# Layer scale on one core: all loads on one DMA ring, all stores on the other, and a first load cut in two

## The chip, the core and the metric

The kernel runs on one core of a Trainium2 chip. Times are device microseconds (us) of one execution. The kernel before takes 121.36 us, the median of 10 runs between 121.07 and 121.44.

## The reference

```python
B, S, D = 1024, 16, 512          # x, y: [B, S, D] bf16; gamma: [D] bf16

def reference(x, y, gamma):
    return x + gamma * y
```

Both inputs and the output are 16,384 rows of 512 bf16 numbers, 16.8 MB each. So 33.6 MB are read from HBM and 16.8 MB written to it, with one multiplication and one addition per element.

## The kernel before

Partition p of 128 holds the rows 128p to 128p + 127 (the rearranged views `xv`, `yv`, `ov`, L38 to L40). The 128 rows of a partition are cut into four pieces of 32 (`PIECE`, L5). One piece is a transfer of 128 partitions with 32 x 512 x 2 bytes = 32 KB each, in all 4 MB. `y_sb` (L45) holds all four pieces of y and later the results, in place; x has two buffers of one piece, `xs` (L46), used in turn.

No scheduler or pool is at work: each engine's order is the order in which the code issues to it, and every wait is written by hand with semaphores. `_take` (L9) waits until a semaphore has reached n and takes n off again.

- **gamma.** ACT loads the row (L65). TensorE multiplies it with a column of ones, so that it stands in all 128 partitions of PSUM (L69), and VectorE (DVE in the profile) copies it into `gamma_sb` (L71).
- **SP's DMA ring** (L75 to L83): x0, x1; then, each after a wait on `s_sp`, x2 and x3 into the buffers that the adds of pieces 0 and 1 have freed; the store of piece 0; after a further wait the store of piece 2.
- **ACT's DMA ring** (L86 to L93): gamma, y0, y1, y2, y3, and, each after a wait on `s_act`, the stores of pieces 1 and 3.
- **VectorE** (L95 to L113), for each piece: wait for y, multiply it by `gamma_sb` in place (L98), wait for x and for the multiplication, add x (L104). The end of the add is told to SP or ACT.
- At the end SP waits for both rings' stores (L115, L116).

The gamma load and the loads x0, x1, y0 and y1 are in the list `first`. L118 to L124 move these instructions to the head of the program, ahead of the barrier with which all engines start.

Of the kernel before, what the change touches and what calls it, by code (L numbers as in the profile page):

```python
# [3 lines left out]

PIECE = 32  # L5
MULT, ADD = mybir.AluOpType.mult, mybir.AluOpType.add


def _take(sem, n, eng):  # L9


    return eng.wait_ge(sem, n).then_inc(sem, -n)  # L12


def kernel(
    tc: tile.TileContext,
    x: bass.AP,
    y: bass.AP,
    gamma: bass.AP,
    out: bass.AP,  # L20
):

    nc = tc.nc
    P = nc.NUM_PARTITIONS
    tc.close()
    tc.compile()  # L29

    xf = x.flatten_outer_dims()
    yf = y.flatten_outer_dims()
    of = out.flatten_outer_dims()
    N, D = xf.shape
    rows = N // P
    n = rows // PIECE
    dt = xf.dtype
    xv = xf.rearrange("(p n) d -> p n d", p=P)  # L38
    yv = yf.rearrange("(p n) d -> p n d", p=P)
    ov = of.rearrange("(p n) d -> p n d", p=P)  # L40

    gamma_row = nc.alloc_sbuf_tensor("gamma_row", [1, D], dt).ap()
    ones_row = nc.alloc_sbuf_tensor("ones_row", [1, P], dt).ap()
    gamma_sb = nc.alloc_sbuf_tensor("gamma_sb", [P, D], dt).ap()
    y_sb = nc.alloc_sbuf_tensor("y_sb", [P, rows, D], dt).ap()  # L45
    xs = [nc.alloc_sbuf_tensor(f"x{i}", [P, PIECE, D], dt).ap() for i in range(2)]  # L46
    gamma_ps = nc.alloc_psum_tensor("gamma_ps", [P, D], mybir.dt.float32).ap()

    sem = nc.alloc_semaphore
    s_gamma, s_ones, s_ps, s_dve = sem("s_gamma"), sem("s_ones"), sem("s_ps"), sem("s_dve")  # L50
    s_x = [sem(f"s_x{c}") for c in range(n)]
    s_y = [sem(f"s_y{c}") for c in range(n)]
    s_sp, s_act = sem("s_sp"), sem("s_act")
    s_out_sp, s_out_act = sem("s_out_sp"), sem("s_out_act")

    def piece(c):
        return slice(c * PIECE, (c + 1) * PIECE)

    first = []

    def load(eng, dst, src, s):
        return eng.dma_start(out=dst, in_=src).then_inc(s, 16)


    first.append(load(nc.scalar, gamma_row, gamma.unsqueeze(0), s_gamma))  # L65
    nc.vector.memset(ones_row, 1.0).then_inc(s_ones, 1)  # L66
    _take(s_ones, 1, nc.tensor)
    _take(s_gamma, 16, nc.tensor)
    nc.tensor.matmul(gamma_ps, ones_row, gamma_row, start=True, stop=True).then_inc(s_ps, 1)  # L69
    _take(s_ps, 1, nc.vector)  # L70
    nc.vector.tensor_copy(out=gamma_sb, in_=gamma_ps).then_inc(s_dve, 1)  # L71
    _take(s_dve, 1, nc.vector)


    first.append(load(nc.sync, xs[0], xv[:, piece(0), :], s_x[0]))  # L75
    first.append(load(nc.sync, xs[1], xv[:, piece(1), :], s_x[1]))
    _take(s_sp, 1, nc.sync)
    load(nc.sync, xs[0], xv[:, piece(2), :], s_x[2])
    _take(s_sp, 1, nc.sync)
    load(nc.sync, xs[1], xv[:, piece(3), :], s_x[3])  # L80
    nc.sync.dma_start(out=ov[:, piece(0), :], in_=y_sb[:, piece(0), :]).then_inc(s_out_sp, 16)
    _take(s_sp, 1, nc.sync)
    nc.sync.dma_start(out=ov[:, piece(2), :], in_=y_sb[:, piece(2), :]).then_inc(s_out_sp, 16)  # L83


    for c in range(n):  # L86
        i = load(nc.scalar, y_sb[:, piece(c), :], yv[:, piece(c), :], s_y[c])
        if c < 2:
            first.append(i)
    _take(s_act, 1, nc.scalar)  # L90
    nc.scalar.dma_start(out=ov[:, piece(1), :], in_=y_sb[:, piece(1), :]).then_inc(s_out_act, 16)
    _take(s_act, 1, nc.scalar)
    nc.scalar.dma_start(out=ov[:, piece(3), :], in_=y_sb[:, piece(3), :]).then_inc(s_out_act, 16)  # L93

    for c in range(n):  # L95
        yt = y_sb[:, piece(c), :]
        _take(s_y[c], 16, nc.vector)
        nc.vector.tensor_tensor(  # L98
            out=yt, in0=yt, in1=gamma_sb[:, None, :].to_broadcast([P, PIECE, D]), op=MULT
        ).then_inc(s_dve, 1)  # L100
        _take(s_x[c], 16, nc.vector)
        _take(s_dve, 1, nc.vector)

        i = nc.vector.tensor_tensor(out=yt, in0=xs[c % 2], in1=yt, op=ADD)  # L104
        if c == 0:
            i.then_inc(s_sp, 1)
        elif c == 1:
            i.then_inc(s_dve, 1)
            _take(s_dve, 1, nc.vector)
            nc.vector.sem_inc(s_sp, 1)  # L110
            nc.vector.sem_inc(s_act, 1)
        else:
            i.then_inc(s_sp if c == 2 else s_act, 1)  # L113

    _take(s_out_sp, 32, nc.sync)  # L115
    _take(s_out_act, 32, nc.sync)  # L116

    main = nc.main_func.blocks[0].instructions  # L118
    names = {i.ins.name for i in first}
    for b in nc.main_func.blocks[1:]:  # L120
        for i in [i for i in b.instructions if i.name in names]:
            b.instructions.remove(i)
    for k, i in enumerate(first):
        main.insert(1 + k, i.ins)  # L124


# [1 line left out]
_INS = ['x', 'y', 'gamma']  # L128
_OUTS = [((1024, 16, 512), 'bfloat16')]


# [23 lines left out]
```

## Time and profile before

| What | Value |
|---|---|
| median of 10 runs | 121.36 us |
| the profiled execution's own time | 121.14 us |
| its span, first to last instruction | 119.8 us |
| VectorE busy | 70.3 us (59%) |
| four multiplications (L98), each | 8.691 us |
| four additions (L104), each | 8.692 us |
| VectorE idle ahead of its first multiplication | 18.0 us |
| moved by DMA | 50.33 MB, 420 GB/s over the span |
| share of 16 DMA engines, SP's ring and ACT's ring | 50.0% and 48.7% |

In the profile the queue q1 is SP's ring and q10 is ACT's. "DMA" in the view by slices is the busy share of the core's 16 DMA engines in tenths, and the GB/s below it are credited to the slice in which a packet starts, which is why they swing from slice to slice. A view by stages gives for each stretch of time the busy time of TensorE, of its weight load, of VectorE and of GpSimd, with the number of instructions, then the granted TensorE clock, the DMA share and GB/s. In the view by time each line has its start and its length in us; a DMA line has the length of the issuing instruction, not that of the transfer.

### The profile page before, as it was taken

What the parts mean: (1) busy time and instruction counts of PE and PEld (TensorE: products, weight loads), DVE (VectorE), ACT (ScalarE), POOL (GpSimd) and SP (SyncE); (2) the same over time, 40 slices, a digit from 0 to 9 for tenths busy, and PEclk for the clock granted to TensorE, in tenths of its full rate; (3) what the DMA queues carried; (4) which work ended last, traced back from release to release, by engine and by line L of the source; (5) the groups of instructions that cost most, each with busy time, mean ns of one, the idle gap of its engine ahead of it and who ended that gap; (6) DMA issues with size and microseconds to landing.
All of it is one profiled execution on the core that took longest, in us unless ns stands there. A gap on an engine that the chain in (4) does not pass through costs nothing. (4 is left out here: it accounts for less than half of the span.)

```text
span 119.8 us, 90 instructions
## 1 busy us (share of the span) xinstructions
PE 0.6 (0%) x1; PEld 0.1 (0%) x1; DVE 70.3 (59%) x10; POOL 0.2 (0%) x4
## 2 busy tenths in 40 slices
PE   0100000000000000000000000000000000000000
PEld 0000000000000000000000000000000000000000
DVE  0100000099999999999899999899999700000000
POOL 0000000000000000000000000000000000000000
DMA  8989898989898989898998989899999898989895
GB/s 263 438 383 492 372 503 361 514 361 514 350 525 350 525 350 525 350 492 383 438 438 383 492 361 438 350 427 427 449 416 460 383 492 361 503 361 503 372 481 219
DMA packets 1730, 50.33 MB, mean 420 GB/s; under 512 B 193, under 2 KB 194, under 8 KB 194
## 3 DMA queue, kind: packets, MB, share of 16 engines
q1 hardware_dynamic: 864, 25.17, 50.0%
q10 hardware_dynamic: 866, 25.17, 48.7%
HBM read 33.56 MB, written 16.78 MB: 420 GB/s over the span
## 5 line engine op out<-in xcount | busy, mean ns | idle before, releaser
L98 DVE TENSOR_TENSOR y_sb<-y_sb,gamma_sb 128x16384 bf16<-128x16384 bf16 x4 | 34.8, 8691 | 18.8 <-DVEq L12 18.8
L104 DVE TENSOR_TENSOR y_sb<-x,y_sb 128x16384 bf16<-128x16384 bf16 x4 | 34.8, 8692 | 0.6
L71 DVE CAST gamma_sb<-gamma_ps 128x512 bf16<-128x512 f32 x1 | 0.7, 692 | 2.7 <-DVEq L12 2.7
L66 DVE MEMSET ones_row<- 1x128 bf16 x1 | 0.2, 165 | 2.7 <-PEq L29 2.7
L69 PE MATMUL gamma_ps<-gamma_row,ones_row 1*128 1x512 bf16 x1 | 0.6, 579 | 4.8 <-PEq L12 4.8
L69 PEld LDWEIGHTS gamma_ps<-gamma_row,ones_row 1*128 1x128 bf16 x1 | 0.1, 100 | 4.8 <-issue 4.8
L139 POOL MEMSET const-bfloat16-1.0<- 128x1 bf16 x1 | 0.1, 102 | 0.0
L139 POOL MEMSET const-uint8-127<- 128x1 uint8 x1 | 0.1, 102 | 0.0
L139 POOL MEMSET const-float32-0.0<- 128x1 f32 x1 | 0.1, 99 | 0.2 <-issue 0.2
L139 POOL MEMSET const-float32-1.0<- 128x1 f32 x1 | 0.1, 99 | 0.0
## 6 DMA issues: line engine op xcount, KB each, us to landing
x<-in_x_dram SPq DMA_DIRECT2D x4, 4096.0 KB, 24.8
y_sb<-in_y_dram ACTq DMA_DIRECT2D x4, 4096.0 KB, 47.1
out_dram<-y_sb ACTq DMA_DIRECT2D x2, 4096.0 KB, 30.3
out_dram<-y_sb SPq DMA_DIRECT2D x2, 4096.0 KB, 42.1
gamma_row<-in_gamma_dram ACTq DMA_DIRECT2D x1, 1.0 KB
```

What stands on the lines that cost most here:

```text
L66: nc.vector.memset(ones_row, 1.0).then_inc(s_ones, 1)
L69: nc.tensor.matmul(gamma_ps, ones_row, gamma_row, start=True, stop=True).then_inc(s_ps, 1)
L71: nc.vector.tensor_copy(out=gamma_sb, in_=gamma_ps).then_inc(s_dve, 1)
L98: nc.vector.tensor_tensor(out=yt, in0=yt, in1=gamma_sb[:, None, :].to_broadcast([P, PIECE, D]), op=MULT).then_inc(s_dve, 1)
L104: i = nc.vector.tensor_tensor(out=yt, in0=xs[c % 2], in1=yt, op=ADD)
L139: nc = _bacc.Bacc("TRN2", target_bir_lowering=False, num_devices=1)
```

## The change

The two rings get lists, `SP` and `ACT`, that a function `ring` works off in order. An x entry has its rows and its place in the buffer `x_sb`, which takes the place of the two x buffers and has their size.

- SP's ring carries all loads: x0, y0, x1, y1, y2, x2, y3, x3. x2 waits for the first add, x3 for the second (a count in `s_add`, one for each add).
- ACT's ring carries gamma and all four stores. The first store also names piece 2, so it waits until three adds are done; stores 1 and 2 follow without a further wait, store 3 waits for the fourth add.
- All stores count on one semaphore, `s_out`, and SP waits once for 64. The adds all count on `s_add`; ACT adds 1 to `s_end` when it has issued its last store.
- The first load of x is two transfers: the partitions 0 to 15 (`FIRST = 16`) and the partitions 16 to 127. Both count on the same semaphore, and the first add waits for 32 on it.
- Ahead of the start barrier stand both parts of x0, y0 and gamma. x1 and y1 are issued behind it.
- VectorE's computing instructions and their order are the same.

The core of the diff:

```diff
-PIECE = 32
+PIECES = [32, 32, 32, 32]
+SP = [('x', 0, 32, 0), ('y', 0, 32), ('x', 32, 64, 32), ('y', 32, 64), ('y', 64, 96), ('x', 64, 96, 0), ('y', 96, 128), ('x', 96, 128, 32)]
+ACT = [('g',), ('s', 0, 32, 2), ('s', 32, 64), ('s', 64, 96), ('s', 96, 128)]
+EARLY = (2, 1)
+FIRST = 16
...
-    xs = [nc.alloc_sbuf_tensor(f"x{i}", [P, PIECE, D], dt).ap() for i in range(2)]
+    x_sb = nc.alloc_sbuf_tensor("x_sb", [P, x_rows, D], dt).ap()
...
+    def ring(eng, what, n_early):
+        known, went = 0, False
+        for k, w in enumerate(what):
+            kind = w[0]
+            need = frees(w) if kind == "x" else pieces_of(w[1], w[2]) + list(w[3:]) if kind == "s" else []
+            need = max((order[c] + 1 for c in need), default=0)
...
+            if need > known:
+                eng.wait_ge(s_add, need)
+                known = need
...
+            elif kind == "x":
+                to = x_sb[:, w[3] : w[3] + w[2] - w[1], :]
+                r = slice(w[1], w[2])
+                if w == x_loads[0]:
+                    i = eng.dma_start(out=to[:FIRST], in_=xv[:FIRST, r, :])
+                    early.append(i.then_inc(s_load[w], 16).ins)
+                    i = eng.dma_start(out=to[FIRST:], in_=xv[FIRST:, r, :])
+                else:
+                    i = eng.dma_start(out=to, in_=xv[:, r, :])
+                i.then_inc(s_load[w], 16)
...
+            else:
+                r = slice(w[1], w[2])
+                i = eng.dma_start(out=ov[:, r, :], in_=y_sb[:, r, :]).then_inc(s_out, 16)
...
+    ring(nc.sync, SP, EARLY[0])
+    ring(nc.scalar, ACT, EARLY[1])
...
-    _take(s_out_sp, 32, nc.sync)
-    _take(s_out_act, 32, nc.sync)
+    nc.scalar.sem_inc(s_end, 1)
+    _take(s_end, 1, nc.sync)
+    _take(s_add, n, nc.sync)
+    _take(s_out, 16 * len(stores), nc.sync)
```

## The prediction

> **What bounds the kernel now.** I read the activity by slices first, then the queues, the stages, and the instructions in order of time.
>
> ```profile
> DMA  8989898989898989898998989899999898989895
> GB/s 263 438 383 492 372 503 361 514 361 514 350 525 350 525 350 525 350 492 383 438 438 383 492 361 438 350 427 427 449 416 460 383 492 361 503 361 503 372 481 219
> ...
> q1 hardware_dynamic: 864, 25.17, 50.0%
> q10 hardware_dynamic: 866, 25.17, 48.7%
> ```
>
> The DMA engines are busy in every slice from the first to the last. The shares of the two queues (SP's and ACT's) add up to 98.7% of 16 engines over 119.8 us, 118.2 us for each engine. The stages say the same; the columns that matter are the DMA share and GB/s at the end of each line.
>
> ```profile
> 0.00:3.00 3.00, 0.00 (x0) 0.00 (x0) 0.17 (x1) 0.20 (x4) 1.00 0.81 262
> 3.00:41.00 38.00, 0.58 (x1) 0.10 (x1) 17.33 (x3) 0.00 (x0) 1.00 1.01 435
> 41.00:60.00 19.00, 0.00 (x0) 0.00 (x0) 18.41 (x4) 0.00 (x0) 1.00 1.01 436
> 60.00:73.00 13.00, 0.00 (x0) 0.00 (x0) 12.85 (x2) 0.00 (x0) 1.00 0.96 413
> 73.00:77.00 4.00, 0.00 (x0) 0.00 (x0) 4.00 (x1) 0.00 (x0) 1.00 1.12 385
> 77.00:96.00 19.00, 0.00 (x0) 0.00 (x0) 17.55 (x3) 0.00 (x0) 1.00 0.99 428
> 96.00:117.00 21.00, 0.00 (x0) 0.00 (x0) 0.00 (x0) 0.00 (x0) 1.00 1.01 437
> 117.00:119.80 2.80, 0.00 (x0) 0.00 (x0) 0.00 (x0) 0.00 (x0) 1.00 0.44 187
> ```
>
> Loads alone (3 to 41 us) run at 435 GB/s, stores alone (96 to 117) at 437, the mixed middle no faster. So neither direction nor mixture matters. One packet is one partition's piece, 32x512 bf16 = 32 KB, and the trace's packet records last 1.213 us in the median, on both queues; call that P. Each of 16 engines has 96 packets (50.33 MB / 32 KB / 16): 96 x 1.213 = 116.4 us. The span is 119.8. The other 3.4 us: the first packet starts 1.0 us after the first instruction, the first round takes some 1.8 us in place of 1.2 (+0.6), packets between 72 and 76 us lose about 1.0, and about 0.8 goes to ends of transfers and the last completion. The loads and the multiply-adds pass each other here:
>
> ```profile
> 24.22 8.69 DVE L98 TENSOR_TENSOR y_sb<-y_sb,gamma_sb 128x16384 bf16<-128x16384 bf16 x1 [18.00 <-DVEq L12]
> 33.06 8.69 DVE L104 TENSOR_TENSOR y_sb<-x,y_sb 128x16384 bf16<-128x16384 bf16 x1
> ...
> 95.13 0.35 ACTq L93 DMA_DIRECT2D out_dram<-y_sb  x1
> ```
>
> DVE works 70.3 us and ends at 95.0; the last store is issued at 95.13 while an earlier one is still moving, and lands with the rest at 119.7. DVE is not the bound. The chain of waits names only the last add, since no engine instruction ends later: what ends last is a DMA queue that never ran dry. So time is what the busiest DMA engine carries, plus 3.4 us. An edit pays only if it empties an engine or slows a packet.
>
> [...] No run here shows a data transfer of fewer than 128 partitions.
>
> **The change, part by part.** Sums are made against the profiled run, 121.14 us (119.8 span + 1.34 around it); the median is 0.22 higher and I add that at the end.
>
> *All loads on SP, in one order; stores on ACT.* Same bytes, same packets: 0 us, as long as no engine runs dry. A piece takes 8 P = 9.7 us. Without the split, pieces would land at about 11.6 (x0), 21.4 (y0), 31.1, 40.9, 50.6 (y2), 60.3 (x2), 70.1 (y3), 79.8 (x3); the fourth landed at 41.1 before too. Each DVE step is 8.69 + 0.15. The first multiply could start at 21.5 in place of 24.2, the adds end near 39, 58, 76 and 94. Three covers: x2's load waits for add 0 with y3 and x3 queued behind it on SP, and y2 covers to 50.6, 12 us of margin; x3's waits for add 1 (58) with y3's load ahead of it moving to 70.1; the held stores wait for add 2 (76), a further 1.0 us to the first packet, and x3's load covers to 79.8, 3 us of margin. If that cover failed, each us of lateness would cost one. The fourth store waits for add 3 (94) behind three stores, 29 us of work. Multiplying earlier buys nothing at the end: the queue is full either way. The issues are 0.33 to 0.46 us each on otherwise idle sequencers, hidden under packets. x1's and y1's loads move behind the start-up barrier, with x0 and y0 (16 P) queued: no cost.
>
> *Store after store on one ring.* In the before the other ring had work when a store ended. Now three ends have no cover. Between 0 and 0.5 us each (last data to last completion at the end of the before took 0.35 us); neighbouring loads on a lone ring near 40.5 us showed under 0.05. I take 0.1 in all, and keep 1.5 as the far end.
>
> *One semaphore for the stores; end marker.* The last two waits of SP were met at 119.71 and 119.78; now one wait follows the last landing: -0.07 us. The marker and the wait for four adds are met around 94, before the end: 0. Taking away per-piece increments and two semaphore instructions of DVE: 0, DVE isn't the bound.
>
> *The first x load as 16 + 112 partitions.* This is what I expect to decide. One more issue (about 0.4 us) lies under the first packets; one more transfer end is about 0.03. A gain at the start: first packets began between 1.01 and 1.69 us, so sooner descriptors may save 0 to 0.7; I take 0.2. [...] I take 6.5 P = 7.9. [...] The late landing also shifts DVE: y0 at 29.3, add 2 ends near 84.0, when the quickest engines have finished x3 at about 83; they idle some 2 us, but are 4 or 5 us ahead of the slowest, so the end doesn't move.
>
> Sum: +7.9 - 0.2 + 0.03 + 0.1 - 0.07 = +7.8 us; 121.14 + 7.8 = 128.9, and with the 0.22 of the median **129.1 us**.
>
> **Rivals.**
> - *[...]the early start wins (ends faster).* If 16 single packets run at full rate, and the 112 too, only the sooner start is left: 0 to 0.7, say 0.45, with -0.07 and +0.13: 121.0 us. It decides as soon as the first transfer holds an engine for less than about 1.4 us (1 P plus the gain). [...]
> - [...]
> - [...]
> - *Store ends block the ring*: +1.5 on top of the first case, 130.6.
>
> **How the numbers follow.** [...] A range of 124.5 to 131.0 leaves out the last two, about 0.2; its top takes in 1.5 us of store ends. About 0.2% can be told from no change here: faster 0.10 and same 0.02[...]; slower 0.88.
>
> **What would show it.** Right: the first round's packets last near 4.9 us, the first slices fall to about 110 GB/s with DMA still busy, y0 lands near 29 and the first multiply starts there, later stretches stay at 435, and the last store is issued near 102. The engines' last completions spread over some 4 us where they spread over 0.6. Wrong: [...] A hole between 76 and 80 us on all engines would mean that the held stores cost something; a gap at each store's end, that completions do.

## The result and the profile after

The changed kernel takes 130.0 us (median of 8 runs, 129.44 to 130.29; a ninth on record, left out of that median, took 129.09), the kernel before 121.32 in the same measurements (median of 29). The ratio is 1.0714, with a 95% interval of 1.0699 to 1.0729: 8.7 us slower. The profiled execution took 130.03 us, with a span of 128.7.

First the view by slices and the queues of the changed kernel (one slice is 3.2 us).

```profile
DMA  9889978999999999989989989989999999999994
GB/s 163 163 204 285 295 194 316 479 407 418 479 397 428 468 397 438 468 377 448 458 367 479 448 377 479 438 387 479 428 397 479 407 418 479 397 428 479 397 428 173
...
q1 hardware_dynamic: 1168, 33.56, 68.2%
q10 hardware_dynamic: 578, 16.78, 30.2%
```

The busy share looks as full as before: 98.4% for the two queues together. But in the first seven slices, 22 us, the same busy engines move only 163 to 316 GB/s. A packet counts as busy for as long as it takes, however slow it is. In the records of the single packets, each engine's first one took 3.2 to 4.6 us and the seven after it 1.6 to 3.1, where a packet of this size usually takes 1.213. The busy share can't show that; the GB/s below it can. The stages show where the slow part ends:

```profile
0.00:3.00 3.00, 0.00 (x0) 0.00 (x0) 0.17 (x1) 0.20 (x4) 1.00 1.26 175
3.00:24.00 21.00, 0.58 (x1) 0.10 (x1) 0.69 (x1) 0.00 (x0) 1.00 0.94 256
24.00:41.00 17.00, 0.00 (x0) 0.00 (x0) 8.91 (x2) 0.00 (x0) 1.00 1.00 432
41.00:60.00 19.00, 0.00 (x0) 0.00 (x0) 17.11 (x2) 0.00 (x0) 1.00 1.01 433
60.00:80.00 20.00, 0.00 (x0) 0.00 (x0) 19.71 (x4) 0.00 (x0) 1.00 1.01 434
80.00:90.00 10.00, 0.00 (x0) 0.00 (x0) 10.00 (x2) 0.00 (x0) 1.00 1.02 439
90.00:117.00 27.00, 0.00 (x0) 0.00 (x0) 13.63 (x2) 0.00 (x0) 1.00 0.99 428
117.00:128.70 11.70, 0.00 (x0) 0.00 (x0) 0.00 (x0) 0.00 (x0) 1.00 0.84 361
```

From 3 to 24 us it is 256 GB/s. From then on it is 428 to 439, through the change from loads to stores near 88 us, until the last stretch, in which the queue empties. All of the loss lies in the load of x0. Its two halves in the list of DMA issues (KB, then us from issue to landing):

```profile
x_sb<-in_x_dram SPq DMA_DIRECT2D x1, 3584.0 KB, 21.7
x_sb<-in_x_dram SPq DMA_DIRECT2D x1, 512.0 KB, 7.1
```

The 16 partitions, an eighth of the piece, landed at 7.1 us; the 112, issued at 0.43, landed at 22.1. The remaining 11 pieces took from 22.09 to the last landing at 128.67: 106.58 us, which is 88 packets per engine at 1.211 us each. DVE followed behind the loads:

```profile
31.94 8.69 DVE L159 TENSOR_TENSOR y_sb<-y_sb,gamma_sb 128x16384 bf16<-128x16384 bf16 x1 [23.81 <-DVEq L25]
40.78 8.69 DVE L168 TENSOR_TENSOR y_sb<-x_sb,y_sb 128x16384 bf16<-128x16384 bf16 x1
...
86.36 17.78 ACTq L123 DMA_DIRECT2D out_dram<-y_sb  x4
95.08 8.69 DVE L168 TENSOR_TENSOR y_sb<-x_sb,y_sb 128x16384 bf16<-128x16384 bf16 x1
```

The stores were released at 86.4, with x3 landing until 90.1: the queue did not run dry at the change.

### The profile page after: what moved, and what is told of

Read it like the earlier page. It is cut to its first block, busy times and chain, and to the rows that moved or that the text cites. A ratio compares the mean times of both kernels' runs of the same rounds, so it can differ in the third digit from the quotient of the medians.

```text
span 128.7 us, 85 instructions
## 1 busy us (share of the span) xinstructions
PE 0.6 (0%) x1; PEld 0.1 (0%) x1; DVE 70.2 (55%) x10; POOL 0.2 (0%) x4
## 5 line engine op out<-in xcount | busy, mean ns | idle before, releaser
L168 DVE TENSOR_TENSOR y_sb<-x_sb,y_sb 128x16384 bf16<-128x16384 bf16 x4 | 34.8, 8692 | 0.6
```

Source lines behind the costliest of these rows:

```text
L168: nc.vector.tensor_tensor(out=yt, in0=xt, in1=yt, op=ADD).then_inc(s_add, 1)
```

## Experiments

The prediction's theory is that the cut along partitions costs the time: packets into part of the 128 partitions take longer. The kernel before has no such transfer, so its trace could not show it. There are two rivals. Either the new order (one ring for the loads, held stores) costs the time, or two transfers in place of one do, however they are cut.

### Without the cut

```diff
-FIRST = 16
...
-                if w == x_loads[0]:
-                    i = eng.dma_start(out=to[:FIRST], in_=xv[:FIRST, r, :])
-                    early.append(i.then_inc(s_load[w], 16).ins)
-                    i = eng.dma_start(out=to[FIRST:], in_=xv[FIRST:, r, :])
-                else:
-                    i = eng.dma_start(out=to, in_=xv[:, r, :])
+                i = eng.dma_start(out=to, in_=xv[:, r, :])
...
-                _take(s_load[w], 32 if w == x_loads[0] else 16, nc.vector)
+                _take(s_load[w], 16, nc.vector)
```

> The changed kernel with its first x load in one piece of 128 partitions; the order on the rings and the held stores stay. [...]x0 lands near 11.6 us instead of 22.1, the rest runs as before it, so 130.0 - 10.5 = 119.5 us, or 121.3 if the order itself gains nothing, as was predicted. Rival (the single load ring and the held stores cost the time): about 129 to 130, first multiply still near 31.

120.17 us, ratio to before 0.9921 (0.9902 to 0.994). The cut costs 130.0 - 120.17 = 9.8 us, and the rest of the change gains 1.2, between the two times that were expected. Stages of this kernel:

```profile
0.00:3.00 3.00, 0.00 (x0) 0.00 (x0) 0.17 (x1) 0.20 (x4) 1.00 0.82 273
3.00:24.00 21.00, 0.58 (x1) 0.10 (x1) 2.83 (x2) 0.00 (x0) 1.00 1.01 435
...
76.00:80.00 4.00, 0.00 (x0) 0.00 (x0) 4.00 (x2) 0.00 (x0) 1.00 0.94 393
80.00:117.00 37.00, 0.00 (x0) 0.00 (x0) 13.56 (x2) 0.00 (x0) 1.00 1.00 432
```

From 3 to 24 us it moves 435 GB/s where the changed kernel moved 256. x0 lands at 12.0 us in place of 22.1, 10.05 us sooner, and the span is 9.9 shorter (118.8). So the new order is not what costs the time. That it gains was not in the prediction.

### The cut alone, in the kernel before

```diff
-    first.append(load(nc.sync, xs[0], xv[:, piece(0), :], s_x[0]))
+    first.append(load(nc.sync, xs[0][:16], xv[:16, piece(0), :], s_x[0]))
+    first.append(load(nc.sync, xs[0][16:], xv[16:, piece(0), :], s_x[0]))
...
-        _take(s_x[c], 16, nc.vector)
+        _take(s_x[c], 32 if c == 0 else 16, nc.vector)
```

> The kernel before with nothing but its first x load as 16 + 112 partitions. [...]slower by 5 to 10 us, 126 to 131[...]. Rival (order and held stores): 121.3, unchanged.

132.07 us, ratio 1.089 (1.0873 to 1.0908): +10.7, above the range of 5 to 10 that was expected, and more than the 9.8 of the changed kernel. So the cut is enough by itself. The stage in which x0 loads:

```profile
3.00:30.00 27.00, 0.58 (x1) 0.10 (x1) 0.69 (x1) 0.00 (x0) 1.00 0.95 261
```

At 261 GB/s it is hardly faster than the changed kernel's 256, although y0 stood on ACT's ring, issued at 0.69 us: its packets did not raise the rate. y0 landed at 36.1 us, where the kernel before had it at 24.1.

### Two transfers, cut along the rows

```diff
-FIRST = 16
+FIRST = 4
...
-                    i = eng.dma_start(out=to[:FIRST], in_=xv[:FIRST, r, :])
+                    i = eng.dma_start(out=to[:, :FIRST, :], in_=xv[:, :FIRST, :])
...
-                    i = eng.dma_start(out=to[FIRST:], in_=xv[FIRST:, r, :])
+                    i = eng.dma_start(out=to[:, FIRST:, :], in_=xv[:, FIRST : w[2], :])
```

> The changed kernel, but the two transfers of the first x load are cut along the rows: all 128 partitions with 4 rows (4 KB each), then all 128 with 28 rows. [...]the same as without a split, give or take 0.5 us for a start that may be earlier: 119.0 to 121.5. Rival (two transfers in place of one, on one semaphore, cost the time however they are cut): near 130.

120.59 us, ratio 0.9951 (0.9934 to 0.9969). The two transfers in the list of DMA issues:

```profile
x_sb<-in_x_dram SPq DMA_DIRECT2D x1, 3584.0 KB, 11.7
x_sb<-in_x_dram SPq DMA_DIRECT2D x1, 512.0 KB, 3.7
```

The same 512 KB go first, but into all 128 partitions. They land 3.7 us after their issue, not 7.1, and the loss is down to 0.4 us over the run without a cut. So it is the cut along partitions that costs, not the second transfer. It gains nothing over the run without a cut either: the whole of x0 landed at 12.15 us, there at 12.04.

### The cut at 64, and at 112

```diff
-FIRST = 16
+FIRST = 64
```

> The changed kernel with the cut at partition 64 instead of 16: 64 + 64 partitions. [...]+9.7 us over the run without a split, 129 to 131, x0's halves landing near 11.5 and 21. Rival (the short first transfer and the odd share of seven partitions are to blame; halves of four partitions per engine are even): within 1 us of the run without a split.

130.75 us, ratio 1.0787 (1.0769 to 1.0805): 10.6 us over the run without a cut, where 9.7 was expected. The halves landed at 12.8 and 23.0. The stage in which x0 loads:

```profile
3.00:22.00 19.00, 0.58 (x1) 0.10 (x1) 0.81 (x2) 0.00 (x0) 1.00 1.01 217
```

217 GB/s is half of 435. Even halves are no better than 16 + 112, so the cost needs neither a short transfer nor unequal parts. The second half took some 10.2 us (23.0 - 12.8); at 435 GB/s its 2 MB would take 4.8.

The cut at 112 has `FIRST = 112`.

> The changed kernel with the cut at 112: the 112 partitions 0 to 111 first, then the last 16. [...]about the same total, 128 to 131. [...]if all engines crawl alike, as the changed kernel's records suggest, all land near 14 to 16.

129.46 us in one run, within the range that was expected. The 112 partitions landed 18.4 us after their issue, when the last of the 16 engines was done; 14 of them had finished between 15.4 and 16.9. So nearly all engines were slow alike, and a little later than the 14 to 16 us that were expected for that.

### Eight transfers of 16 partitions, neighbours or eight apart

```diff
-FIRST = 16
...
-                    i = eng.dma_start(out=to[:FIRST], in_=xv[:FIRST, r, :])
-                    early.append(i.then_inc(s_load[w], 16).ins)
-                    i = eng.dma_start(out=to[FIRST:], in_=xv[FIRST:, r, :])
+                    for j in range(8):
+                        q = slice(16 * j, 16 * j + 16)
+                        i = eng.dma_start(out=to[q], in_=xv[q, r, :])
+                        if j < 7:
+                            early.append(i.then_inc(s_load[w], 16).ins)
...
-                _take(s_load[w], 32 if w == x_loads[0] else 16, nc.vector)
+                _take(s_load[w], 128 if w == x_loads[0] else 16, nc.vector)
```

The other kernel differs from it only in `q = slice(j, None, 8)`.

> The first x load as eight transfers of 16 neighbouring partitions each (0 to 15, 16 to 31, ...). [...]+29 us on the run without a split, about 149[...]. Rival (the cost is one of short transfers of 16 partitions, or of their number): the same as with the partitions taken eight apart.

> The first x load as eight transfers of 16 partitions each, eight apart (0, 8, 16, ...; then 1, 9, 17, ...). [...]+9.7 us on the run without a split, about 130. Rival (short transfers, or their number): the same time as the eight blocks of neighbours.

Neighbours: 145.34 us. Eight apart: 130.76, each in one run. Both have the same number of transfers, partitions and bytes; only which partitions go together differs. While x0 is loading, the stage of the neighbours is

```profile
3.00:37.00 34.00, 0.58 (x1) 0.10 (x1) 0.86 (x2) 0.00 (x0) 1.00 0.98 123
```

and that of the partitions eight apart

```profile
3.00:22.00 19.00, 0.58 (x1) 0.10 (x1) 0.86 (x2) 0.00 (x0) 1.00 1.01 214
```

123 and 214 GB/s are a little over a quarter and about a half of the full 435. The packets' records add up to the times: a packet took 4.39 us with the neighbours and 2.56 with the partitions eight apart, where one of a whole piece takes 1.213. Eight rounds of 4.39 - 1.213 make 25.4 us and eight of 2.56 - 1.213 make 10.8; measured over the run without a cut, it is 25.2 and 10.6, where 29 and 9.7 were expected. With the neighbours the engines end x0 up to 1.8 us apart. Why the two choices cost what they cost is not shown.

This is the sharpest of the tests, since only the choice of partitions changed. One thing it can't separate: each partition of x0 has its own rows in HBM, so the addresses that are read together change too. The 64 and the partitions eight apart ran alike (217 and 214 GB/s) although they read different rows together. Whether the limit lies where HBM is read or where SBUF is written is not shown: no run tests either side by itself.

### Where the order's 1.2 us come from

Two runs separate the order of the loads from the holding of the stores. One takes the hold out of the run without a cut:

```diff
-ACT = [('g',), ('s', 0, 32, 2), ('s', 32, 64), ('s', 64, 96), ('s', 96, 128)]
+ACT = [('g',), ('s', 0, 32), ('s', 32, 64), ('s', 64, 96), ('s', 96, 128)]
```

> The run without a split, and the first store no longer held for the third add: stores go out as each piece is added, between the loads. Theory A (stores among loads cost the 1.2 us by which the new order beats the kernel before; its slow packets at 72 to 76 us are that): about 121.2, slow packets near the first stores. Theory B (the order of the loads, not the holding, gives the gain): 120.2, as without a split.

130.52 us, ratio 1.0779 (1.0748 to 1.081). Neither theory had this: 10.35 us are lost to something else. Its stages and the DVE lines:

```profile
3.00:39.00 36.00, 0.58 (x1) 0.10 (x1) 17.78 (x3) 0.00 (x0) 1.00 1.00 430
39.00:45.00 6.00, 0.00 (x0) 0.00 (x0) 4.09 (x2) 0.00 (x0) 1.00 1.01 360
45.00:109.00 64.00, 0.00 (x0) 0.00 (x0) 39.66 (x5) 0.00 (x0) 1.00 1.00 433
109.00:118.00 9.00, 0.00 (x0) 0.00 (x0) 8.69 (x1) 0.00 (x0) 1.00 0.00 0
```

```profile
80.18 8.69 DVE L162 TENSOR_TENSOR y_sb<-x_sb,y_sb 128x16384 bf16<-128x16384 bf16 x1 [10.50 <-DVEq L24]
90.98 8.69 DVE L153 TENSOR_TENSOR y_sb<-y_sb,gamma_sb 128x16384 bf16<-128x16384 bf16 x1 [2.11 <-DVEq L24]
109.26 8.69 DVE L162 TENSOR_TENSOR y_sb<-x_sb,y_sb 128x16384 bf16<-128x16384 bf16 x1 [9.59 <-DVEq L24]
```

With all loads on one ring and stores on the other, the engines took packets from both in turn: from 60 to 80 us the loads' queue held 48.7% of the engines' time and the stores' 48.6%. Each early store pushed loads back: x2 landed at 79.9 and x3 at 109.0 (60.6 and 80.1 with the hold). DVE waited 10.5 and 9.6 us for them. While it did the last add there was nothing left to move: nine us without a byte, and only then the fourth store. In this order the hold is what keeps the queue full to the end. Theory A has a part in it: 39 to 45 us, around the first store, ran at 360 GB/s in place of 430, which costs (430 - 360) / 430 x 6 = 1.0 us.

The other run holds the stores in the kernel before and leaves its loads alone:

```diff
+    _take(s_sp, 1, nc.sync)
     nc.sync.dma_start(out=ov[:, piece(0), :], in_=y_sb[:, piece(0), :]).then_inc(s_out_sp, 16)
-    _take(s_sp, 1, nc.sync)
...
-        if c == 0:
+        if c < 2:
             i.then_inc(s_sp, 1)
-        elif c == 1:
+        elif c == 2:
...
-            i.then_inc(s_sp if c == 2 else s_act, 1)
+            i.then_inc(s_act, 1)
```

> The kernel before, both rings' loads as they were, but the first two stores held until the third add, like the others in the changed kernel. Theory A (mixing costs): about 120.2. Theory B (order of the loads): 121.3, as before.

120.33 us, ratio 0.9926 (0.9903 to 0.9949): -0.9 us, as theory A has it. As far as the intervals can tell, the hold accounts for the whole gain, and the new order of the loads adds nothing to it that shows. The kernel before was profiled once more:

> The kernel before once more, for a second profile. If the slow packets at 72 to 76 us belong to the kernel they are there again, about 1 us for each DMA engine; if they were an accident of that execution they are gone or elsewhere, and the span is near 119.

121.15 us, span 119.8. Its stage of 73 to 77 us,

```profile
73.00:77.00 4.00, 0.00 (x0) 0.00 (x0) 4.00 (x1) 0.00 (x0) 1.00 1.09 385
```

and the same stage with the stores held,

```profile
73.00:77.00 4.00, 0.00 (x0) 0.00 (x0) 3.77 (x1) 0.00 (x0) 1.00 1.07 459
```

In so short a stretch the GB/s swing, because packets are credited where they start; share and GB/s have to be read together. 385 at a share of 1.09 is 353 GB/s for a full share, and 459 at 1.07 is 429, as in the stage of loads alone (435 at 1.01). The 393 of 76 to 80 us in the run without a cut has a share of 0.94, so it is no such dip. The slow packets of the first profile are thus there again in the second, load packets of up to 2.0 us just ahead of the first store's packets (76.3). They are gone with the hold, which lets the first stores begin as the last load ends. So these slow packets belong to the kernel and not to one execution, and they are about the size of the gain.

## Why the prediction was right, point by point

**What bounds the kernel: right.** A full DMA queue set the end in every run but the one without the hold. From x0's landing to the end the changed kernel lost nothing, at 1.211 us a packet.

**The cut at 16: right in cause, too small.** The term was +7.9 us and measured 9.8. Its size, 6.5 packet times for x0, was the author's estimate, which no trace of the kernel before showed; that the cut along partitions is what costs is shown by the runs without it (120.17) and with the cut along the rows (120.59). Why the packets slow down, no run shows.

In the records of the changed kernel the first packet of an engine took 3.2 to 4.6 us (2.6 to 3.8 packet times; the sign I gave was 4.9 us), and the seven took 14.7 to 16.1 us (12.2 to 13.3 packet times) on every engine. So the first 16 partitions cost less than the sign had it, and yet the whole of x0 landed (22.09 - 12.04) / 1.213 = 8.3 packet times later than without the cut, where I took 6.5. As the engines were slow alike, their last completions lie 1.3 us apart (127.35 to 128.67), not the 4 I announced. How the 112 partitions are shared among the engines, and why not one of their packets ran at the full rate (the shortest took 1.6 us), stays open.

**The order and the hold at 0 us: wrong by 1.2 us.** The step that failed is the reading of the kernel before. I saw the packets between 72 and 76 us lose about 1.0 us and put it into the fixed 3.4 us of every version. I took the stages at 435 and 437 GB/s to mean that mixing loads and stores is free, although the mixed stage of 73 to 77 us beside them stood at 385 GB/s with a DMA share of 1.12. The hold takes the loss away (-0.9 in the kernel before, and a span of 118.8 without the cut in place of 119.8). Why the first store slows the loads for a moment is not shown. It isn't the mixture alone: the kernel before with the cut also mixes them, and 83 to 90 us, around its first store, ran at 435 GB/s. What spared it is open too.

The two misses have opposite signs, 1.9 too little and 1.2 too much. That the total, +7.8, came so near to the measured +8.7 is in part luck.

**The covers: right.** None failed; after the three adds the last load had 2 to 4 us left to land. But I priced only a failure of the hold, as the lateness of one wait, and did not ask what the hold is for. Without it the order of this kernel loses 10.35 us.

**Store after store on one ring, 0.1 us: right in effect.** Eleven pieces at 1.211 us a packet leave nothing for the ends of transfers, so the 1.5 us of the rival are excluded.

**Early start, -0.2 us: not there.** The first packet began 1.01 us after the first instruction in both kernels, and cutting along the rows brought no gain. After the last landing SP has one wait in place of two, which saves the 0.07 us as stated.

**The rivals.** The early start wins (121.0): excluded by 130.0, though without the cut the change did make the kernel faster (120.17), as far as the runs tell by the held stores; the first packet began no earlier. Store ends block the ring (130.6): excluded by the 1.211 us a packet, as said above.

**What would show it.** The first multiply was announced near 29 and came at 31.9, the last store near 102 and came at 103.8; no hole between 76 and 90 us. The slices I announced at 110 GB/s stood at 163 and more. That view credits a packet to the slice in which it starts, and engines that were done with their first packet had already begun on the 112. With nothing but blocks of 16 the rate was 123.

The best version here is the changed kernel without the cut, 120.17 us. The kernel before with held stores, 120.33, can't be told from it.

## What to carry to other kernels

In all four cuts along partitions tried here, 16 + 112, 112 + 16, 64 + 64 and eight times 16 (neighbours or eight apart), the loads into fewer than 128 partitions kept the 16 DMA engines busy (a share of 0.92 to 1.03) at 123 to 262 GB/s in place of 435, and held up what was queued behind them: 9 to 25 us in all. The cut along the rows cost 0.4. So, as far as these runs go, cut a transfer along the free dimension and keep all partitions in each part. Read the DMA busy share together with GB/s: the blocks of neighbours had a share of 0.98 at 123 GB/s. With the loads on one ring and the stores on the other, stores that were ready early took the place of loads that compute waited for, 10.5 and 9.6 us, and the kernel lost 10.35. Here holding them until the last load was 2 to 4 us from landing was enough; other lengths of the hold were not tried.

## What the runs showed that was not expected

- Packets of 32 KB took 4.39 us in blocks of 16 neighbouring partitions, 2.56 with 16 partitions eight apart and 1.213 in whole pieces: 3.6 times and 2.1 times as long.
- The transfer of 112 partitions ran at 262 GB/s by itself (3 to 15 us of the run with 112 first), on nearly all engines alike.
- A first store among loads cost 0.8 to 1.0 us on all 16 engines in three profiles (two of the kernel before, one without the hold), by the excess of the packets' records over 1.213 us. With the hold it was 0.0 to 0.4 us, in the mean of the engines, in all eight profiles, and nothing in the kernel before with the cut.
